# A planner's costs replaced by times read from the trace: block-sparse attention and a mixture of experts on one core

## The chip, the core and the metric

The kernel runs on one core of a Trainium2 chip. Five engines run their own instruction streams in order: TensorE (PE, with its weight loads PEld), VectorE (DVE), ScalarE (ACT), GpSimd (POOL) and SyncE (SP, which here only issues DMAs). They meet at semaphores. The metric is the device time of one execution in microseconds; lower is better.

## The reference

Attention over 4 batches x 8 heads, 768 positions of width 64, in blocks of 32: a query block sees its neighbours, the first and the last block, and three sampled blocks. Its output is the input x (3072 tokens x 512) of eight experts, whose outputs are weighted by a matrix P that is balanced by eight rounds of row and column division.

```
scores = np.where(mask, scale * q @ k.T, -1e9)
attn = exp(scores - max) / (sum + 1e-9);  x = attn @ v        # 3072 x 512
P = balance(exp(x @ w_gate - max))                            # 8 rounds, 3072 x 8
for e in range(8):
    h = np.maximum(x @ w1[e], 0.0)                            # 512 -> 1024
    out += P[:, e:e+1] * (h @ w2[e])                          # 1024 -> 512
```

## The kernel before

Every matrix operand is split into a high and a low half-precision part, and a product is three matmuls (high x high, high x low, low x high). The first 416 us are attention, whose order is written out by hand. After that come 32 items, item i = 4e + b being expert e on batch b. An item has two stages. Stage 1 (x @ w1) and stage 2 (h @ w2) each use a Strassen-like scheme of 7 products p = 0..6, and from expert 2 on four of stage 1's products are themselves split into 7 (L1620, groups of six matmuls of 192 columns; L1591 are the unsplit groups of six of 384 columns). Stage 2 is L1943, groups of twelve matmuls of 256 columns.

PE writes a bank of PSUM (p for stage 1, y for stage 2), DVE and ACT empty it and add it to sums in SBUF, and the same bank then takes the next product, so that a PE group often waits for the reader of the group before: L1573 (ACT), L1564, L1657, L1673, L1686, L1695 (DVE) in stage 1, L1970 (ACT) and L1982 (DVE) in stage 2. The relu'd sums are split again into h tiles: high parts by ACT (L1820), low parts by DVE (L1811, L1826, L1835) or POOL (L1809). Differences of sums are L1851, on DVE or POOL.

Stage 2's results of experts 2 to 6 are added to DRAM by an accumulating DMA that POOL issues (L2003, accd<-acc).

**A round of weights.** For each expert's w1 and w2 the kernel needs one power of two as a scale. ACT takes eight maxima (L352), DVE joins them (L441, ma_w<-mx_w), SP sends the 128 maxima to DRAM (L1316, peak_d<-ma_w) and reads them back to all partitions (L1320, peaks<-peak_d), and DVE makes the scale from them (L447 to L454, six small instructions in one job called power). Then ACT and DVE split the weights (L1346 and L1351). There are 15 such rounds after attention.

**Who sets the order.** Class Plan takes 7951 jobs with their dependencies, buffers and assumed durations, and runs through them in an assumed time: an engine that is free takes the ready job that is due first (PE: the one with the earliest place in a table of due times). What it yields is the program's order on each engine; at run time every engine keeps to that order, and only semaphores hold it. So an assumed time that is wrong doesn't change what is computed, but it places an instruction too early or too late in its engine's queue. Assumed are: LAT between engines, DMA_LAND from a DMA's last byte to its reader, MARGIN on durations. EASE, SHIFT, SLK and SLK2 set the due times of PE groups and of bank readers. A job with `port=True` doesn't run beside another such job in the plan: these are DVE's and POOL's jobs that read two operands from SBUF.

Of the kernel before, what the change touches and what calls it, by code (L numbers as in the profile page):

```python
# [32 lines left out]
PORDER = (0, 1, 5, 6, 3, 4, 2)  # L33
TWO = (6, 3, 1, 2)
NB1, NH, NPAIRS, NU, NACC = 5, 24, 9, 4, 3
SLK, SLK2, SHIFT, EASE, SOON = 1.5, 2.0, 9.5, 0.3, 120.0
SLK3 = 20.0
PREP0, PREP1, PREPD = 100, 190, 50
TWO1 = ()
ADDS = 2  # L40
LOFT = 31
# [16 lines left out]
class Job:  # L58
    __slots__ = (
        "engs", "fn", "deps", "take", "drop", "pt", "dl", "stream", "kb",  # L60
        "rush", "lag", "port", "wait", "succ", "start", "end", "eng", "ready", "seq", "free",
    )


class Plan:
    LAT = 0.2
    DMA_RATE, DMA_LAND = 190.0, 2.0
    MARGIN = 1.0

    def __init__(self, shelf):  # L70
        self.shelf = shelf
# [31 lines left out]
        self.jobs.append(j)  # L103
        return j

    def dma(self, fn, kb, deps=(), take=(), drop=(), dl=None, eng="SP"):
        return self.job({eng: 0.08 if eng == "SP" else 1.0}, fn, deps, take, drop, dl=dl, kb=kb)

    def engine(self, nc):
        return nc.gpsimd if self.current == "POOL" else nc.vector  # L110

    def span(self, j):
        if j.kb:
            return j.kb / self.DMA_RATE + self.DMA_LAND
        return min(j.engs.values())

    def deadlines(self):
# [11 lines left out]
    def run(self):  # L129
        self.deadlines()  # L130
        ENG = ("PE", "DVE", "ACT", "POOL", "SP", "-")
        free = {e: 0.0 for e in ENG}
        dma_free = 0.0
# [14 lines left out]
        wait = {}  # L148
# [40 lines left out]
        def start(j, e, t):  # L189
            nonlocal dma_free, port_free, left  # L190
            for h in j.take:
                if h.tile is None:
                    _, h.tile = items[h.pool].pop(0)
            j.start, j.eng = t, e
            dur = j.engs[e]
            if e not in ("PE", "SP", "-"):
                dur *= self.MARGIN
            if j.kb:
                begin = max(t + dur, dma_free)
                dma_free = begin + j.kb / self.DMA_RATE  # L200
                j.end = dma_free + self.DMA_LAND
                free[e] = t + dur
            else:
                j.end = t + dur
                free[e] = j.end
                if j.port:
                    port_free = j.end
            if e == "-":
                free[e] = 0.0
            for h in j.drop:  # L210
                h.users.discard(j)
                if not h.users:
                    items[h.pool].append((j.end + self.LAT, h.tile))
                    items[h.pool].sort(key=lambda x: x[0])
            if j.stream:
                pos[j.stream] += 1
            for s in j.succ:
                s.wait -= 1
                if not s.wait:
                    s.ready = max(  # L220
                        d.end + (self.LAT if d.eng != "-" and not (d.eng in s.engs and not d.kb) else 0.0)
                        for d in s.deps
                    ) + s.lag
                    cand.append(s)
            cand.remove(j)
            self.done.append(j)
            left -= 1

        EPSI = 1e-7
        while left:  # L230
            moved = False
            for e in ENG:
                while free[e] <= t + EPSI:
# [20 lines left out]
                    else:  # L254
                        for j in sorted(ok, key=lambda j: (j.dl, j.seq)):
                            end = t + j.engs[e]
# [42 lines left out]
def tile_sparse_attention_moe(  # L299
# [11 lines left out]
    nc = tc.nc  # L311
# [990 lines left out]
    def scale_jobs(which, e, loaded):  # L1302
        cell = {}

        def make():
            cell["steps"] = scale_steps(which, e)
            wr["s", which, e] = wr["s", which]

        made = job({"-": 0.0}, make, (loaded[1],))
        parts = [  # L1310
            job({"ACT": 0.81}, lambda k=k: cell["steps"][0][k](), (made, loaded[k // 4]))
            for k in (4, 5, 6, 7, 0, 1, 2, 3)
        ]
        whole = job({"DVE": 0.16}, lambda: cell["steps"][1](), parts)
        out_ = plan.dma(
            lambda: nc.sync.dma_start(out=peak_d[which - 1], in_=cell["steps"][4]), 1, (whole,)  # L1316
        )

        def back():
            nc.sync.dma_start(  # L1320
                out=peaks[which - 1],
                in_=peak_d[which - 1].rearrange("p one -> (p one)").unsqueeze(0).to_broadcast([P, P]),
            )
            wr["all", which] = peaks[which - 1]

        in_ = plan.dma(back, 64, (out_,))
        power = job({"DVE": 1.2}, lambda: cell["steps"][3](), (in_,))
        scaled[which, e] = power
        return parts, power
# [569 lines left out]
    def stage2(i, t0, length):  # L1899
# [99 lines left out]
        if e < NE - 1:  # L1999
            for j in range(2):  # L2000
                if fresh and e:
                    accstore[i, j] = plan.dma(
                        lambda j=j: nc.gpsimd.dma_start(  # L2003
                            out=accd[b][j], in_=pieces[j].tile, accum_op=ALU.add
                        ),
                        768, tuple(writes[j]) + (accstore[i - B, j],), drop=(pieces[j],), eng="POOL",
                    )
                else:
                    accstore[i, j] = plan.dma(
                        lambda j=j: nc.sync.dma_start(out=accd[b][j], in_=pieces[j].tile), 768,  # L2010
                        tuple(writes[j]), drop=(pieces[j],),
                    )
# [126 lines left out]
```

## Time and profile before

| | us |
|---|---|
| median of 3 runs | 2186.05 (2181.29 to 2190.05) |
| the profiled execution | 2180.49, span 2178.6 |
| PE busy | 2117.1 (97%) |
| DVE busy | 1714.8 (79%) |
| ACT busy | 1443.4 (66%) |
| POOL busy | 1202.2 (55%) |
| chain that ended last: PE 87%, DVE 6%, DMA 4% | |
| of it peak_d<-ma_w 2%, peaks<-peak_d 1% | |

The span is the time from the first to the last instruction of the profiled execution. PE's busy time is the union of its matmuls, so what is missing to the span is time in which PE had nothing running. The chain is followed back from the last instruction to whatever released it; a DMA on it means that at that place everything later stood behind that DMA. Times in the rows are counted from the span's start.

### The profile page before, as it was taken

How to read it: one execution, taken by the hardware profiler on the slowest of the kernel's cores; microseconds unless marked ns; L12 is line 12 of the kernel's file. 1: busy time of each engine (PE TensorE's matmuls, PEld its weight loads, DVE VectorE, ACT ScalarE, POOL GpSimd, SP SyncE). 2: the span in 40 equal slices, each digit the busy share in tenths (PEclk: the TensorE clock that was granted, in tenths of full speed). 3: DMA queues.
4: the chain of work that ended last, by engine and by line, in shares of the span. 5: the costliest groups of instructions: out<-in, count | busy, mean ns of one | idle time of the engine just before them, and what ended most of it. 6: DMA issues, size and time to landing. Idle time of an engine off the chain costs nothing.

```text
span 2178.6 us, 51353 instructions
## 1 busy us (share of the span) xinstructions
PE 2117.1 (97%) x20605; PEld 1708.3 (78%) x20605; DVE 1714.8 (79%) x3053; ACT 1443.4 (66%) x2773; POOL 1202.2 (55%) x1383
## 2 busy tenths in 40 slices
PE   6999999899999999999999999999999999999999
PEld 3777776667777778788888888888888888887887
DVE  8888888678787878777887688768876887787776
ACT  4788888776668656765676667656766676666442
POOL 5556768555445536554664466545654664475433
PEclk9999999999999999999999999999999999999999
DMA  7667966433456544564456454545464545455421
GB/s 171 142 135 163 211 132 137 141 106 104 154 176 193 168 158 131 151 150 110 120 139 150 110 148 128 133 110 143 118 148 110 146 131 132 110 163 147 139 95 66
DMA packets 228195, 300.57 MB, mean 138 GB/s; under 512 B 137436, under 2 KB 157812, under 8 KB 227956
## 3 DMA queue, kind: packets, MB, share of 16 engines
q1 hardware_dynamic: 221632, 265.80, 42.6%
q0 software_dynamic: 5760, 31.46, 8.7%
q8 instruction: 161, 2.64, 0.5%
q14 instruction: 78, 0.64, 0.1%
q10 hardware_dynamic: 564, 0.03, 0.0%
HBM read 198.15 MB, written 67.64 MB: 122 GB/s over the span
## 4 chain that ended last, share of the span: by engine, by line
PE 87%; DVE 6%; DMA 4%; issue 1%; ACT 1%; POOL 0%; SPq 0%; DVEq 0%; ACTq 0%; POOLq 0%
PE y L1943 38%; PE p L1591 21%; PE p L1620 14%; PE u L966 4%; PE t L904 2%; PE t L901 2%; PE m L868 2%; PE m L871 2%; DMA peak_d<-ma_w 2%; DMA peaks<-peak_d 1%; DVE top L877 1%; DMA qt<-qs 1%; PE u L997 0%; DVE pair L1851 0%; DVE pl L919 0%
## 5 line engine op out<-in xcount | busy, mean ns | idle before, releaser
L1943 PE MATMUL y<-w2p,h 128*128 128x256 f16 x8064 | 971.5, 273 | 5.1 <-ACT w2p L1346 2.1
L1943 PEld LDWEIGHTS <-h 128*128 128x128 f16 x8064 | 787.4, 98 | 126.3 <-issue 3.9
L1809 POOL TENSOR_TENSOR h<-pair,h 128x384 f16<-128x384 f32 x413 | 414.8, 1025 | 442.0 <-ACT h L1820 371.6
L1820 ACT ACTIVATE h<-pair 128x384 f16<-128x384 f32 x640 | 313.2, 515 | 79.4 <-DVE pair L1851 25.6
L1591 PE MATMUL p<-arena 128*128 128x384 f16 x1728 | 324.5, 327 | 0.6 <-DVE pair L1564 0.6
L1564 DVE SCALAR_TENSOR_TENSOR pair<-p,pair 128x384 f32<-128x384 f32 x384 | 212.9, 555 | 137.0 <-PE p L1591 132.4
L1805 ACT ACTIVATE pair<-pair 128x384 f32<-128x384 f32 x384 | 196.6, 518 | 165.9 <-DVE pair L1564 134.1
L1982 DVE SCALAR_TENSOR_TENSOR acc<-y,spare,acc 128x256 f32<-128x256 f32 x408 | 201.6, 496 | 114.1 <-PE y L1943 112.8
L1591 PEld LDWEIGHTS <-arena 128*128 128x128 f16 x1728 | 167.1, 98 | 83.1 <-issue 2.4
L877 DVE TENSOR_REDUCE top<-m 128x1 f32<-128x768 f32 x192 | 181.9, 951 | 48.7 <-PE m L871 47.8
L1591 PE MATMUL p<-attic 128*128 128x384 f16 x1152 | 216.4, 328 | 3.5 <-DVE pair L1564 3.5
L909 ACT ACTIVATE pe<-t,qk 128x768 int32<-128x768 f32 x192 | 172.3, 899 | 70.7 <-PE t L904 63.2
L1620 PEld LDWEIGHTS <-loft 128*128 128x128 f16 x2304 | 198.4, 98 | 25.2 <-issue 11.1
L1591 PEld LDWEIGHTS <-attic 128*128 128x128 f16 x1344 | 131.2, 98 | 73.5 <-issue 7.1
L1620 PE MATMUL p<-loft 128*128 128x192 f16 x1728 | 176.6, 246 | 1.9 <-DVE u L1657 1.1
L1970 ACT ACTIVATE acc<-y,spare 128x256 f32<-128x256 f32 (+1 forms) x180 | 97.7, 543 | 99.8 <-PE y L1943 99.2
L1851 POOL TENSOR_TENSOR pair<-pair,pair 128x384 f32<-128x384 f32 x114 | 126.4, 1119 | 59.1 <-DVE pair L1851 51.7
L1334 POOL TENSOR_TENSOR raw_w<-raw_w 128x256 f32<-128x256 f32 (+1 forms) x150 | 127.8, 862 | 56.1 <-DVE attic L1351 24.2
L1573 ACT ACTIVATE u<-p 128x384 f32<-128x384 f32 x216 | 105.3, 488 | 71.7 <-PE p L1620 68.4
L1809 POOL TENSOR_TENSOR h<-u,h 128x384 f16<-128x384 f32 x116 | 112.8, 978 | 67.4 <-ACT h L1820 60.1
L868 PE MATMUL m<-kt,qt 128*128 128x512 f16 (+1 forms) x384 | 126.6, 330 | 10.4 <-DMA kt<-ks 7.0
L1573 ACT ACTIVATE pair<-p 128x384 f32<-128x384 f32 x168 | 82.0, 489 | 82.0 <-PE p L1620 38.9
(236 smaller groups left out, 3937.7 us busy)
## 6 DMA issues: line engine op xcount, KB each, us to landing
arena<-xd SPq DMA_DIRECT2D x128, 384.0 KB, 3.3
attic<-xd SPq DMA_DIRECT2D x96, 384.0 KB, 3.3
loft<-xsd SPq DMA_DIRECT2D x96, 384.0 KB, 4.5
accd<-acc POOLq DMA_DIRECT2D x40, 768.0 KB, 8.5
raw_w<-in_moe_w_dram SPq DMA_DIRECT2D x28, 1024.0 KB, 5.2
accd<-acc SPq DMA_DIRECT2D x16, 768.0 KB, 4.2
acc<-accd SPq DMA_DIRECT2D x16, 768.0 KB, 5.1
xd<-loft SPq DMA_DIRECT2D x28, 384.0 KB, 2.9
```

The costliest lines, as they stand in the source:

```text
L868: nc.tensor.matmul(sc[:, lo:hi], lhsT=qt[:, 0, c], rhs=ka[:, lo:hi], start=True, stop=False)
L877: nc.vector.tensor_reduce(out=tops[n][:, c : c + 1], in_=sc[:, :S], axis=AX.X, op=ALU.max)
L909: nc.scalar.activation(pe, sc[:, :S], AF.Exp, bias=EXP_SHIFT, scale=qk[n // 2][3])
L1564: lambda: nc.vector.scalar_tensor_tensor(out=out_(), in0=bank_(), scalar=HDOWN, in1=add(), op0=ALU.mult, op1=ALU.add),
L1573: lambda: nc.scalar.activation(out_(), bank_(), AF.Relu if relu else AF.Copy, scale=HDOWN),
L1591: nc.tensor.matmul(bk.tile[:, :TH], lhsT=w1p[p][:, l, kc, fs], rhs=xp[p][:, r, kc], start=(fresh and kc == 0 and m == 0), stop=(kc == KH - ...
L1620: nc.tensor.matmul(bk.tile[:, c * HT : (c + 1) * HT], lhsT=lhs(l, c), rhs=rhs(rr), start=(fresh and c == 0 and m == 0), stop=(m == 2), ski ...
L1805: return job({"ACT": 0.52}, lambda: nc.scalar.activation(view(), view(), AF.Relu), dep)
L1809: nc.gpsimd.tensor_tensor(out=out_, in0=x, in1=y, op=ALU.subtract)
L1820: lambda: nc.scalar.activation(h.tile[:, 0], src(), AF.Relu if relu else AF.Copy),
L1943: nc.tensor.matmul(py, lhsT=hh[i, p, kc].tile[:, l, tsl], rhs=w2p[p][:, r, kc], start=(old is None and kc == 0 and m == 0), stop=(kc == h2 ...
L1982: lambda dst=dst, src=src, t=t: nc.vector.scalar_tensor_tensor(out=dst(), in0=src(), scalar=pwe[e][:, t : t + 1] if e else 1.0, in1=dst(), ...
```

## The change

The planner's assumed times are replaced. LAT falls from 0.2 to 0.06 us; every duration on DVE, ACT and POOL is multiplied by 1.08; an engine is free again 0.08 (DVE), 0.1 (ACT) or 0.06 us (POOL) before its job ends; a DMA has its own landing time, 8.0 us for peak_d<-ma_w, 5.2 for peaks<-peak_d, 4.5 for the accumulating DMA and 2.0 for the rest. The due times change through SLK, SLK2, SHIFT and EASE. PREP0 is used only for products in TWO1, which is empty. No job is added or removed: the same 7951 jobs are put in another order, and 51 more of those that DVE or POOL may take fall to DVE (25 from L1809 to L1811, 26 of L1851), while of the preparation of x two, net, go the other way. Attention's order is the same on every engine.

```diff
--- before.py
+++ after.py
@@ -33,9 +33,9 @@
 PORDER = (0, 1, 5, 6, 3, 4, 2)
 TWO = (6, 3, 1, 2)
 NB1, NH, NPAIRS, NU, NACC = 5, 24, 9, 4, 3
-SLK, SLK2, SHIFT, EASE, SOON = 1.5, 2.0, 9.5, 0.3, 120.0
+SLK, SLK2, SHIFT, EASE, SOON = 2.5, 5, 11, 0.2, 120.0
 SLK3 = 20.0
-PREP0, PREP1, PREPD = 100, 190, 50
+PREP0, PREP1, PREPD = 60, 190, 50
 TWO1 = ()
 ADDS = 2
 LOFT = 31
@@ -58,14 +58,15 @@
 class Job:
     __slots__ = (
         "engs", "fn", "deps", "take", "drop", "pt", "dl", "stream", "kb",
-        "rush", "lag", "port", "wait", "succ", "start", "end", "eng", "ready", "seq", "free",
+        "rush", "lag", "port", "land", "wait", "succ", "start", "end", "eng", "ready", "seq", "free",
     )
 
 
 class Plan:
-    LAT = 0.2
+    LAT = 0.06
+    OVER = {"DVE": 0.08, "ACT": 0.1, "POOL": 0.06}
     DMA_RATE, DMA_LAND = 190.0, 2.0
-    MARGIN = 1.0
+    MARGIN = 1.08
 
     def __init__(self, shelf):
         self.shelf = shelf
@@ -103,15 +104,17 @@
         self.jobs.append(j)
         return j
 
-    def dma(self, fn, kb, deps=(), take=(), drop=(), dl=None, eng="SP"):
-        return self.job({eng: 0.08 if eng == "SP" else 1.0}, fn, deps, take, drop, dl=dl, kb=kb)
+    def dma(self, fn, kb, deps=(), take=(), drop=(), dl=None, eng="SP", land=None):
+        j = self.job({eng: 0.08 if eng == "SP" else 1.0}, fn, deps, take, drop, dl=dl, kb=kb)
+        j.land = self.DMA_LAND if land is None else land
+        return j
 
     def engine(self, nc):
         return nc.gpsimd if self.current == "POOL" else nc.vector
 
     def span(self, j):
         if j.kb:
-            return j.kb / self.DMA_RATE + self.DMA_LAND
+            return j.kb / self.DMA_RATE + j.land
         return min(j.engs.values())
 
     def deadlines(self):
@@ -198,11 +201,11 @@
             if j.kb:
                 begin = max(t + dur, dma_free)
                 dma_free = begin + j.kb / self.DMA_RATE
-                j.end = dma_free + self.DMA_LAND
+                j.end = dma_free + j.land
                 free[e] = t + dur
             else:
                 j.end = t + dur
-                free[e] = j.end
+                free[e] = j.end - self.OVER.get(e, 0.0)
                 if j.port:
                     port_free = j.end
             if e == "-":
@@ -1313,7 +1316,7 @@
         ]
         whole = job({"DVE": 0.16}, lambda: cell["steps"][1](), parts)
         out_ = plan.dma(
-            lambda: nc.sync.dma_start(out=peak_d[which - 1], in_=cell["steps"][4]), 1, (whole,)
+            lambda: nc.sync.dma_start(out=peak_d[which - 1], in_=cell["steps"][4]), 1, (whole,), land=8.0
         )
 
         def back():
@@ -1323,7 +1326,7 @@
             )
             wr["all", which] = peaks[which - 1]
 
-        in_ = plan.dma(back, 64, (out_,))
+        in_ = plan.dma(back, 64, (out_,), land=5.2)
         power = job({"DVE": 1.2}, lambda: cell["steps"][3](), (in_,))
         scaled[which, e] = power
         return parts, power
@@ -2003,7 +2006,7 @@
                         lambda j=j: nc.gpsimd.dma_start(
                             out=accd[b][j], in_=pieces[j].tile, accum_op=ALU.add
                         ),
-                        768, tuple(writes[j]) + (accstore[i - B, j],), drop=(pieces[j],), eng="POOL",
+                        768, tuple(writes[j]) + (accstore[i - B, j],), drop=(pieces[j],), eng="POOL", land=4.5,
                     )
                 else:
                     accstore[i, j] = plan.dma(
```

What this does to the order is seen at three places. In the rows of the changed kernel lines up to L106 are one higher and the lines of the jobs three higher (L441 is L444, L447 is L450). The numbers behind names are buffers.

DVE in the last round (w2 of expert 7), before: the rows that stand behind L441 up to L447, which waits for peaks.

```order
L1982 SCALAR_TENSOR_TENSOR acc_8056<-y_8016,spare_24582,acc_8056 128x256
L1835 TENSOR_TENSOR h_8028<-p_8010,h_8028 128x384
L1982 SCALAR_TENSOR_TENSOR acc_8056<-y_8017,spare_24582,acc_8056 128x256
L1851 TENSOR_TENSOR pair_8047<-p_8010,pair_8047 128x384
L1564 SCALAR_TENSOR_TENSOR pair_8042<-p_8013,pair_8042 128x384
L1564 SCALAR_TENSOR_TENSOR pair_8042<-p_8014,pair_8042 128x384
L1686 SCALAR_TENSOR_TENSOR pair_8050<-p_8012,u_8052 128x2x192
L1826 SCALAR_TENSOR_TENSOR h_8022<-pair_8042,h_8022 128x384
L1982 SCALAR_TENSOR_TENSOR acc_8056<-y_8015,spare_24582,acc_8056 128x256
L1564 SCALAR_TENSOR_TENSOR pair_8048<-p_8013,pair_8048 128x384
L1564 SCALAR_TENSOR_TENSOR p_8013<-p_8013,pair_8043 128x384
L447 TENSOR_REDUCE ma_w_7_26855<-peaks_8069 128x1
```

The same place in the changed kernel: the first five and the last six of the rows behind L444, with 20 left out.

```order
L1567 SCALAR_TENSOR_TENSOR pair_8046<-p_8012,pair_8046 128x384
L1567 SCALAR_TENSOR_TENSOR p_8013<-p_8013,pair_8049 128x384
L1567 SCALAR_TENSOR_TENSOR p_8012<-p_8012,pair_8049 128x384
L1862 SCALAR_TENSOR_TENSOR u_8053<-p_8013,pair_8045 128x384
L1862 SCALAR_TENSOR_TENSOR u_8054<-p_8012,pair_8045 128x384
...
L1985 SCALAR_TENSOR_TENSOR acc_8056<-y_8015,spare_24653,acc_8056 128x256
L1698 SCALAR_TENSOR_TENSOR pair_8049<-p_8014,u_8051 128x2x192
L1567 SCALAR_TENSOR_TENSOR pair_8042<-p_8010,pair_8042 128x384
L1567 SCALAR_TENSOR_TENSOR p_8010<-p_8010,pair_8043 128x384
L1985 SCALAR_TENSOR_TENSOR acc_8056<-y_8016,spare_24653,acc_8056 128x256
L450 TENSOR_REDUCE ma_w_7_26851<-peaks_8069 128x1
```

Before, 11 rows stand between the maximum and the row that waits for the round trip; now 30 do.

SP at the same round, before: peak_d and peaks are the round trip, raw_w, xd and xsd are loads of weights and of x.

```order
L475 DMA attic<-xd_77 128x1536
L1498 DMA loft<-xsd_8071 128x1536
L475 DMA arena<-xd_77 128x1536
L1316 DMA peak_d_8067<-ma_w_7_26855 128x1
L1320 DMA peaks_8069<-peak_d_8067 128x128
L475 DMA arena<-xd_77 128x1536
```

SP there in the changed kernel.

```order
L478 DMA attic<-xd_77 128x1536
L1501 DMA loft<-xsd_8071 128x1536
L1319 DMA peak_d_8067<-ma_w_7_26851 128x1
L478 DMA attic<-xd_77 128x1536
L1501 DMA loft<-xsd_8071 128x1536
L478 DMA arena<-xd_77 128x1536
L1323 DMA peaks_8069<-peak_d_8067 128x128
```

Before, the read stands straight behind the write; now three loads of x stand between them.

POOL behind the accumulating DMA of item 12's first half (expert 3, batch 0), before; raw_w is a weight buffer.

```order
L2003 DMA accd_0_8058<-acc_8055 128x1536
L1809 TENSOR_TENSOR h_8026<-pair_8042,h_8026 128x384
L1809 TENSOR_TENSOR h_8030<-pair_8050,h_8030 128x384
L1809 TENSOR_TENSOR h_8021<-pair_8047,h_8021 128x384
L1851 TENSOR_TENSOR pair_8048<-pair_8048,pair_8050 128x384
```

The same DMA in the changed kernel.

```order
L2006 DMA accd_0_8058<-acc_8055 128x1536
L1812 TENSOR_TENSOR h_8023<-pair_8043,h_8023 128x384
L1337 TENSOR_TENSOR raw_w<-raw_w 128x512
L1854 TENSOR_TENSOR pair_8044<-pair_8044,pair_8042 128x384 x2
L1812 TENSOR_TENSOR h_8032<-pair_8043,h_8032 128x384
L1812 TENSOR_TENSOR h_8026<-pair_8042,h_8026 128x384
L1812 TENSOR_TENSOR h_8027<-pair_8044,h_8027 128x384
L1812 TENSOR_TENSOR h_8022<-pair_8049,h_8022 128x384
```

The DMA is followed by three h rows and a difference before, and by one h row, a weight sum (L1337), two differences and four h rows now.

## Rows read from the trace of the kernel before

**Rows 1.** Windows before and from the plan: stretch, length, busy per engine, granted clock.

```profile
0.00:416.00 416.00, 388.35 (x5324) 278.00 (x5324) 344.33 (x561) 321.60 (x441) 265.58 (x397) 0.99 0.71 158
416.00:2179.00 1763.00, 1728.71 (x15281) 1430.27 (x15281) 1370.51 (x2493) 1121.82 (x2332) 936.63 (x986) 1.00 0.47 133
```

**Rows 2.** PE's waits, 416 to 2179: waiter, releaser, total us, times, longest.

```profile
PE p L1620 <- DVE pair L1695: 7.7, 5, 2.9
PE p L1620 <- DVE u L1657: 7.6, 8, 1.4
PE p L1591 <- DVE pair L1564: 4.1, 2, 3.5
PE y L1943 <- ACT w2p L1346: 2.1, 1, 2.1
PE y L1943 <- DVE w2p L1351: 1.9, 2, 1.3
PE p L1591 <- DVE pair L1851: 1.5, 1, 1.5
PE p L1620 <- ACT pair L1573: 1.1, 1, 1.1
```

**Rows 3.** DVE's waits, 416 to 2179, the one row on L447.

```profile
DVE ma_w L447 <- DMA peaks<-peak_d: 36.4, 10, 6.7
```

**Rows 4.** The two small DMAs: form, count, KB each, median us to landing.

```profile
peaks<-peak_d SPq DMA_DIRECT2D x15, 64.0 KB, 5.4
...
peak_d<-ma_w SPq DMA_DIRECT2D x15, 0.5 KB, 7.3
```

**Rows 5.** Timeline of DVE, last round: start us, us, instruction, idle before.

```profile
1970.21 0.15 DVE L441 TENSOR_REDUCE ma_w<-mx_w 128x1 f32<-128x8 f32 x1
...
1978.08 0.56 DVE L1564 SCALAR_TENSOR_TENSOR p<-p,pair 128x384 f32<-128x384 f32 x1
1982.98 0.28 DVE L447 TENSOR_REDUCE ma_w<-peaks 128x1 f32<-128x128 f32 x1 [4.34 <-DMA peaks<-peak_d]
```

**Rows 6.** Chain of waits, 1955 to 1992: start us, us, what.

```profile
1970.38 7.11 DMA peak_d<-ma_w
...
1977.50 5.38 DMA peaks<-peak_d
```

**Rows 7.** Timeline of PE at three of the gaps.

```profile
1551.28 0.66 PE L1620 MATMUL p<-arena,loft 128*128 128x192 f16 x6 [2.35 <-DVE pair L1695]
...
1769.22 0.66 PE L1620 MATMUL p<-arena,loft 128*128 128x192 f16 x6 [1.56 <-DVE pair L1695]
...
1984.60 0.66 PE L1620 MATMUL p<-arena,loft 128*128 128x192 f16 x6 [2.94 <-DVE pair L1695]
```

**Rows 8.** Windows at the four drops of the granted clock.

```profile
448.40:455.30 6.90, 5.17 (x17) 2.48 (x17) 6.85 (x13) 4.74 (x9) 1.85 (x1) 0.56 0.48 176
905.80:909.20 3.40, 2.04 (x10) 1.33 (x10) 3.40 (x7) 3.40 (x7) 0.43 (x1) 0.63 0.50 202
1550.90:1554.30 3.40, 3.02 (x20) 2.54 (x20) 2.84 (x5) 3.26 (x5) 0.90 (x1) 0.63 0.42 107
1984.40:1987.80 3.40, 3.20 (x22) 2.61 (x22) 3.40 (x7) 3.40 (x5) 0.89 (x1) 0.63 0.44 120
```

**Rows 9.** Timeline of POOL, DVE and PE around one accumulating DMA.

```profile
1179.28 0.88 POOL L2003 DMA_DIRECT2D accd<-acc  x1 [2.55 <-PE y L1943]
...
1179.89 2.94 POOL L1809 TENSOR_TENSOR h<-pair,h 128x384 f16<-128x384 f32 x3
...
1180.19 3.07 DVE L1851 TENSOR_TENSOR pair<-pair,pair 128x384 f32<-128x384 f32 x1
...
1183.18 1.01 DVE L1657 SCALAR_TENSOR_TENSOR u<-p,pair 128x384 f32<-128x384 f32 x2
1183.78 0.41 PE L1620 MATMUL p<-loft,attic 128*128 128x192 f16 x3 [1.02 <-DVE u L1657]
```

**Rows 10.** DVE's h rows on L1811, from 420 us: count, busy us, mean ns, idle before.

```profile
L1811 DVE SCALAR_TENSOR_TENSOR h<-pair,h 128x384 f16<-128x384 f32 x99 | 77.2, 786 | 3.9 <-ACT h L1820 3.9
```

## The prediction, made before the result was known

> **What bounds the kernel now.** I read the page first: PE is busy for 97% of the span and makes up 87% of the chain that ended last, so the kernel is bound by matmul work that the change neither adds to nor takes from. What can move is PE's idle time, and the time that it spends at half clock. So the second view is windows at the seam between the hand-ordered attention and the planned part [rows 1]. Attention's order is the same on all engines, so its 27.7 us of idle PE stay. In the planned part PE is busy for 1728.7 of 1763.0 us: 34.3 us idle is nearly all that any order could win.
>
> The third view, PE's waits, says where they are [rows 2]: a few dozen gaps of 0.4 to 3.5 us, nearly all released by DVE, though DVE is busy for only 78% of that stretch (1370.5 of 1763.0). An engine with free time that releases late is itself held, so the fourth view is DVE's own waits [rows 3]: L447, the first instruction of the power job, holds DVE's queue ten times for 36.4 us in all, up to 6.7 us at once, until the second of two small DMAs has landed. The DMA view has their medians, 7.3 us for the write and 5.4 us for the read back [rows 4]. The planner of before counted about 2 us for each landing, so it placed power some 8 us too early in DVE's queue. The timeline of the last round shows what follows [rows 5]: DVE ends its last row before power at 1978.64, sits idle for 4.34 us, and the six small rows follow. The chain runs through just these two DMAs, 7.11 and 5.38 us [rows 6]. Behind power stands L1695, which empties the bank that PE needs next, and PE sits idle until 1984.60, for 2.94 us [rows 7].
>
> **What the waits on L447 cost PE.** I add the gaps that lie right behind such a hold. Three waits on L1695: 2.35 + 1.56 + 2.94 = 6.85 us [rows 7] (the row's total of 7.7 has two small ones more that lie elsewhere). Both waits on L1564, 4.1 us, behind the first round's hold of 6.7 us [rows 2, 3]. At about 906 the stage 2 of expert 2 waits for its freshly split weights, 2.1 us for the high and 1.3 us for the low part, and once, behind another round's hold, PE waits 1.1 us for ACT [rows 2]. Sum: 6.85 + 4.1 + 3.4 + 1.1 = 15.5 us.
>
> Four of these gaps are followed by a lower granted clock: windows of 6.9 and three times 3.4 us have means of 0.56 and 0.63 of full speed [rows 8], which is the lower level (1.2 GHz) but for the windows' edges. PE was idle just ahead and for part of each. Busy time multiplied by the missing share of the clock is 5.17 x 0.44 + (2.04 + 3.02 + 3.20) x 0.37 = 2.3 + 3.0 = 5.3 us.
>
> **The change part by part.** The new landing times, 8.0 and 5.2, are close to the medians. In the new order 30 DVE rows stand between L441 and L447 in the last round, where 11 stood. At about 0.56 us each [rows 5] they are 17 us of DVE work, against a round trip of 7.11 + 5.38 = 12.5 us [rows 6]; DVE's waits for PE come on top. Every later round of w2 has 30 rows too, so these holds should go whole. The first round has 24 rows, 13.4 us against 12.7 by the medians: thin. The rounds of w1 get 25 to 28 rows (it was 21 to 24), some 15 us, and may still hold DVE; before, no gap of PE followed theirs directly. What hides the longer round is that weights are needed later: in the new order the first split of w2 and its user still have several PE groups between them, about as many as before. SP now issues three loads of x between write and read. Each can hold SP's queue while x is still being read by PE, which delays the read at worst until the next group of PE is done; the spare is 17 - 12.5 = 4.5 us. I count 15.5 + 5.3 = 20.8 us as removed, less 2 for what the first round and expert 2 may keep: 19 us. Both ends: 10 (half of the gaps are the matmuls' own lateness and come back) and 21.
>
> The other waits: LAT, MARGIN, the overlaps and the due times reshuffle every queue. What is left after 15.5 of 34.3 us is mainly the eight waits on L1657, 7.6 us, and one of 1.5 on L1851 [rows 2]; the rest is small gaps and the end of the kernel, where the order still closes with the same 26 groups of stage 2. Five of the waits on L1657 look alike [rows 9]. POOL waits 2.55 us to issue an accumulating DMA, then runs three h rows back to back (1179.89 to 1182.83). A DVE difference that also reads two SBUF operands starts at 1180.19 and lasts 3.07 us. L1657, behind it, starts at 1183.18, and PE has been idle for 1.02 us. The new order has such places too: behind the same DMA more POOL rows stand in a row, though no DVE row with two SBUF operands stands beside them there; elsewhere one does. I take this term as 0, with -8 (all gone) and +12 (twice as many and longer) as ends.
>
> The 51 jobs that fall to DVE are 51 x 0.79 = 40 us of it [rows 10], about what the holds give back (36.4), so DVE stays near 78%. If that cover is gone, DVE is at 80%, and the bank readers come later by a fraction of a row; I keep it within the +12.
>
> The Trainium skill, page "SBUF — State Buffer", section "SBUF: two separate sides", says of these two engines that their shared pair of ports is locked for one instruction, and that whoever comes second blocks fully for that instruction. By that rule a DVE row would lose one POOL row at most, about 1 us. In this trace it lost three [rows 9]: the measurement decides. By the rule alone the slower rival below would fall away; by the row it lives.
>
> Sum: 2180.5 - 19 = 2161.5 for an execution like the profiled one. That one was 5.6 us faster than the median of the three runs; from the median the sum is 2167. I take the middle, 2164 us. Its own range, from the ends 10 and 21 and from -8 to +5 of the small waits, is 2152 to 2177.
>
> **The rivals.**
> First, the gaps move instead of going. PE's waits on L1695 are replaced by waits behind POOL's bursts, or the power job, now late, makes the splits late. For it: the new order has up to five POOL rows ready behind an accumulating DMA, and 40 of these DMAs. Against: only eight waits on L1657 in 40 before, each about 1 us. If twelve more such gaps of 1.2 us come, 14 us of the 19 are lost: 2181 us.
>
> Second, the times fit so much better that the collisions go as well. For it: DVE's holds make the run drift from the plan, and the collision of [rows 9] is one that the plan forbids (`port`). Against: POOL's waits for DVE's sums stay. Then 8 + 2 us more are won: 2154 us.
>
> Third, slower: a DVE row with two SBUF operands meets a burst of five POOL rows instead of three. The hold grows from 3.07 to about 5 us and PE's gap from 1.02 to 3 us; gaps of 2.35 and 2.94 us were followed by a lower clock [rows 7, 8], about 1.1 us more each. With two such places per expert in five experts: 10 x 4.1 = 41, less the 7.6 there now, less the 19 won: +14 us, 2200 us. It decides from about ten such gaps on. For it: the new order puts a low part on DVE and a difference of sums at the end of such a burst once per item or two. Against: the plan keeps these jobs apart.
>
> **How the numbers follow.** The forecast has 0.63, the second rival 0.12, the first 0.15, the third 0.10. A measurement of this kernel can tell 0.5%, 11 us, from no change: faster is below 2175, slower above 2197. The forecast falls into "no change" with one part in twenty or so of its chance, and the first rival lies there with nearly all of its own, while the second is faster: faster 0.72, same 0.18, slower 0.10. For 8 times in 10 I go from 2150, a little under the second rival, to 2184, beyond the first.
>
> **What would show it.** In the changed kernel's profile: the wait of DVE on L450 (L447 of before) falls from 36.4 us to under 15, and what is left is in the rounds of w1. PE's waits on L1698 and L1567 (L1695 and L1564 of before) fall from 11.8 to under 3 us. The granted clock stays at full speed but for one drop at most after 430 us. PE's idle time from 416 us on falls from 34 to about 19 us, and the two small DMAs' share of the chain from 3% to under 1%. The forecast is wrong if PE's total of waits on DVE's L1660 (L1657) is above 15 us, if DVE rows of 3 us and more number above ten, or if stage 2 waits for w2p at every expert.

## The result, and the profile after

The changed kernel takes 2158.8 us (median of 4 runs, 2156.38 to 2162.62) beside 2183.67 for the kernel before on the same chip (2180.62 to 2190.05): a ratio of 0.9884, interval 0.9856 to 0.9912. That is 25 us or 1.2% less, and the runs of the two kernels don't overlap. The profiled execution took 2156.38 us with a span of 2154.6, 24.0 us shorter than the profiled span before. Line numbers of the new kernel are 3 higher: L447 is now L450, L1620 is L1623, L1657 is L1660, L1695 is L1698.

The windows at the same seam, with the same columns as [rows 1]:

```profile
0.00:416.00 416.00, 388.72 (x5342) 278.42 (x5342) 345.66 (x564) 321.29 (x441) 265.50 (x397) 1.00 0.71 159
416.00:2155.00 1739.00, 1720.79 (x15263) 1425.83 (x15263) 1390.99 (x2539) 1110.60 (x2332) 897.03 (x937) 1.00 0.52 135
```

Up to the end of the last instruction, PE's idle time after 416 us fell from 33.9 to 17.8 us and its busy time by 7.9 us. Not all of this is the change's. Attention, whose order is the same, runs 1.8 us ahead in this execution: the first matmul on xn starts at 416.16 us instead of 417.92, and 18 matmuls that stood behind 416 us now stand before it (both traces have 20605). From that matmul on, before and after:

```profile
417.92:2178.60 1760.68, 1727.99 (x15263) 1429.68 (x15263) 1369.53 (x2489) 1121.82 (x2332) 936.63 (x986) 1.00 0.47 133
416.16:2154.60 1738.44, 1720.79 (x15263) 1425.83 (x15263) 1390.89 (x2538) 1110.60 (x2332) 897.03 (x937) 1.00 0.52 135
```

So the planned part gave 22.2 of the 24.0 us, for the same 15263 matmuls: 15.0 of idle time (32.7 to 17.7) and 7.2 of busy time.

PE's waits after 416 us (waiter, releaser, total us, times, longest), to be held against [rows 2]:

```profile
PE p L1623 <- DVE pair L1854: 3.4, 1, 3.4
PE p L1623 <- DVE u L1660: 3.2, 6, 2.0
PE y L1946 <- DVE h L1829: 2.6, 6, 0.5
PE p L1623 <- DVE pair L1676: 1.8, 1, 1.8
PE p L1594 <- DVE pair L1567: 1.4, 2, 0.7
...
PE p L1623 <- DVE pair L1698: 0.6, 1, 0.6
```

DVE's own wait at the start of power, which was 36.4 us in ten holds [rows 3]:

```profile
DVE ma_w L450 <- DMA peaks<-peak_d: 2.3, 1, 2.3
```

The waits on L1698 and L1567, 11.8 us before, are 2.0; those on the fresh w2p are gone. The hold is left once, in a round of w1. The two small DMAs themselves show no sign of being faster (form, count, KB, median us to landing; before [rows 4]):

```profile
peaks<-peak_d SPq DMA_DIRECT2D x15, 64.0 KB, 8.5
...
peak_d<-ma_w SPq DMA_DIRECT2D x15, 0.5 KB, 8.7
```

These medians, 17.2 us together where it was 12.7, are over the landings that the profile knows: in after those of 3 writes and 7 reads of 15, and all seven are reads of w1's rounds. In before the reads of the same seven rounds had a median of 8.7 us. The DMAs no longer show because more DVE work stands in front of power. The timeline of DVE in the last round, where before 4.34 us of idle stood ahead of power [rows 5]:

```profile
1940.36 0.15 DVE L444 TENSOR_REDUCE ma_w<-mx_w 128x1 f32<-128x8 f32 x1
...
1959.35 0.48 DVE L1985 SCALAR_TENSOR_TENSOR acc<-y,spare,acc 128x256 f32<-128x256 f32 x1 [0.28 <-PE y L1946]
1959.75 0.28 DVE L450 TENSOR_REDUCE ma_w<-peaks 128x1 f32<-128x128 f32 x1
```

From the maxima to power it is now 19.4 us of DVE's time, and power follows the row before it without a gap.

Of gaps of 1 us and more PE has four after 416 us, where it had 13: 3.40, 2.03, 1.80 and 1.07. The first two, from PE's timeline (start us, us, instruction, idle before):

```profile
897.38 2.44 PE L1623 MATMUL p<-loft 128*128 128x192 f16 x18 [3.40 <-DVE pair L1854]
...
1974.15 0.66 PE L1623 MATMUL p<-loft,attic 128*128 128x192 f16 x6 [2.03 <-DVE u L1660]
```

The window at the first of them holds the one drop of the granted clock after 430 us, where there were four [rows 8]:

```profile
897.00:900.40 3.40, 3.02 (x23) 2.91 (x23) 2.89 (x5) 1.54 (x3) 3.00 (x3) 0.65 0.15 58
```

Neither gap is a wait for a DMA. At the first, DVE works without a pause from 890.87 us on: a split of w2 (1.27 us), the job that weighs an expert's tokens (1.7 us) and seven other rows stand ahead of the one that PE needs, L1854. It is the round of w2 of expert 2, where before had its gaps at about 906 [rows 8]. DVE's timeline just ahead of the second gap:

```profile
1968.91 0.20 DVE L1468 TENSOR_SCALAR pc<-iw,iw 128x1 f32<-128x1 f32 x1
1969.15 3.80 DVE L1470 TENSOR_SCALAR pcb<-inv_v,pc 128x4 f32<-128x4 f32 x1
...
1973.56 0.55 DVE L1660 SCALAR_TENSOR_TENSOR u<-p,pair 128x384 f32<-128x384 f32 x1
```

and POOL's at the same time:

```profile
1968.41 0.88 POOL L2006 DMA_DIRECT2D accd<-acc  x1 [0.59 <-PE p L1623]
1969.02 1.21 POOL L1812 TENSOR_TENSOR h<-u,h 128x384 f16<-128x384 f32 x1
1969.89 1.20 POOL L1812 TENSOR_TENSOR h<-pair,h 128x384 f16<-128x384 f32 x1
1970.77 1.28 POOL L1854 TENSOR_TENSOR pair<-pair,pair 128x384 f32<-128x384 f32 x1
1971.72 1.19 POOL L1812 TENSOR_TENSOR h<-pair,h 128x384 f16<-128x384 f32 x1
```

A DVE row over four columns (part of the same weighing job), 0.23 us at its shortest, runs for 3.80 us, as long as a train of POOL rows without gaps, and the reader of PE's bank stands behind it. Such a place I call a meeting below. It is of the kind of [rows 9].

### The profile page after: what moved, and what is told of

It reads as the page before. It is cut to its first block, busy times and chain, and to the rows that moved or that the text cites. A ratio compares the mean times of both kernels' runs of the same rounds, so it can differ in the third digit from the quotient of the medians.

```text
span 2154.6 us, 51373 instructions
## 1 busy us (share of the span) xinstructions
PE 2109.5 (98%) x20605; PEld 1704.2 (79%) x20605; DVE 1736.7 (81%) x3102; ACT 1431.9 (66%) x2773; POOL 1162.5 (54%) x1334
## 4 chain that ended last, share of the span: by engine, by line
PE 91%; DVE 5%; issue 1%; ACT 1%; DMA 1%; POOL 1%; SPq 0%; ACTq 0%; POOLq 0%; DVEq 0%
PE y L1946 40%; PE p L1594 23%; PE p L1623 14%; PE u L969 4%; PE t L904 2%; PE t L907 2%; PE m L871 2%; PE m L874 2%; DVE top L880 1%; DVE h L1829 1%; DVE pcb L1470 1%; DMA qt<-qs 1%; PE u L1000 0%; DVE pl L922 0%; ACT pe L912 0%
## 5 line engine op out<-in xcount | busy, mean ns | idle before, releaser
L1812 POOL TENSOR_TENSOR h<-pair,h 128x384 f16<-128x384 f32 x386 | 396.4, 1036 | 456.3 <-ACT h L1823 381.8
L1567 DVE SCALAR_TENSOR_TENSOR pair<-p,pair 128x384 f32<-128x384 f32 x384 | 213.5, 556 | 153.5 <-PE p L1594 150.0
L1623 PEld LDWEIGHTS <-loft 128*128 128x128 f16 x2304 | 199.5, 98 | 18.2 <-issue 6.7
L1623 PE MATMUL p<-loft 128*128 128x192 f16 x1728 | 180.3, 247 | 5.4 <-DVE pair L1854 3.4
L1337 POOL TENSOR_TENSOR raw_w<-raw_w 128x256 f32<-128x256 f32 (+1 forms) x150 | 131.0, 884 | 33.4 <-DVE attic L1354 14.3
L871 PE MATMUL m<-kt,qt 128*128 128x512 f16 (+1 forms) x384 | 127.2, 331 | 10.3 <-DMA kt<-ks 7.0
L926 POOL TENSOR_SCALAR pl<-pe 128x768 f16<-128x768 uint16 x112 | 96.3, 864 | 70.7 <-ACT pe L912 68.6
L904 PE MATMUL t<-qt,kt 128*128 128x512 f16 (+1 forms) x384 | 125.5, 327 | 2.8 <-DVE top L880 2.1
```

Of the source, the lines that this page charges most:

```text
L871: nc.tensor.matmul(sc[:, lo:hi], lhsT=qt[:, 0, c], rhs=ka[:, lo:hi], start=True, stop=False)
L904: nc.tensor.matmul(sc[:, lo:hi], lhsT=kt[:, 0, c], rhs=qa[:, lo:hi], start=True, stop=False)
L1567: lambda: nc.vector.scalar_tensor_tensor(out=out_(), in0=bank_(), scalar=HDOWN, in1=add(), op0=ALU.mult, op1=ALU.add),
L1623: nc.tensor.matmul(bk.tile[:, c * HT : (c + 1) * HT], lhsT=lhs(l, c), rhs=rhs(rr), start=(fresh and c == 0 and m == 0), stop=(m == 2), ski ...
L1812: nc.gpsimd.tensor_tensor(out=out_, in0=x, in1=y, op=ALU.subtract)
```

## The experiments

The theory was: DVE's queue is held at power by the two small DMAs, PE waits for the bank readers behind it, and the new landing times put enough DVE work ahead of it. The rivals were that the other new times or the new due times make the gain, and that any new order of 7951 jobs falls somewhere in a spread, by luck. Each ratio is to the kernel before, run in the same rounds on the same chip (its medians 2183.67 to 2188.28 us). "Hold" is DVE's wait at power, "idle" PE's idle time after 416 us, in the profiled execution. That one can lie off the median: e9's is 7.5 us above it, e7's and e11's are the quickest of ten.

| kernel | us | ratio, interval | idle | hold (times) |
|---|---|---|---|---|
| before | | 1 | 33.9 | 36.4 (10) |
| after | 2158.80 | 0.9884, 0.9856 to 0.9912 | 17.8 | 2.3 (1) |
| e5: order of before, no wait | 2163.43 | 0.9893, 0.9866 to 0.9920 | 23.6 | 1.4 (1) |
| e1: landing times alone | 2159.68 | 0.9871, 0.9851 to 0.9891 | 22.1 | 0 |
| e2: all but landing times | 2218.55 | 1.0149, 1.0120 to 1.0179 | 62.6 | 41.2 (8) |
| e7: e2's order, no wait | 2183.45 | 0.9996, 0.9984 to 1.0007 | 36.5 | 5.7 (2) |
| e6: order of after, no wait | 2157.05 | 0.9859, 0.9838 to 0.9879 | 18.7 | 0 |
| e3: durations and distances alone | 2240.11 | 1.0254, 1.0239 to 1.0269 | 75.7 | 65.8 (14) |
| e4: due times alone | 2166.07 | 0.9912, 0.9898 to 0.9927 | 23.9 | 25.5 (7) |
| e10: landing, durations, distances | 2170.07 | 0.9920, 0.9903 to 0.9938 | 27.3 | 2.2 (2) |
| e11: landing and due times | 2181.90 | 0.9974, 0.9958 to 0.9990 | 33.8 | 0.3 (1) |
| e8: after and port on the weighing | 2150.34 | 0.9843, 0.9829 to 0.9858 | 11.8 | 0 |
| e9: e1 and port on the weighing | 2182.00 | 0.9976, 0.9952 to 0.9999 | 36.6 | 0 |
| e12: e11 and port on the weighing | 2174.13 | 0.9941, 0.9924 to 0.9959 | 28.2 | 1.5 (3) |

**The wait alone (e5).** The order of before stays as it is; power reads a constant tile that was loaded long ago, so it waits for no read back, and the scales are those of the constant. The DMAs still run.

```diff
-            wr["all", which] = peaks[which - 1]
+            wr["all", which] = ident
```

> The kernel before in its own order, but the scale's first instruction reads a constant 128x128 tile instead of the tile that the round trip brings, so it waits for no DMA; the DMAs still run. (The scales are those of the constant.) Theory 1: all ten holds of DVE go, and with them PE's 15.5 us of gaps and the drops of the clock: about 2162 us, 18 to 24 us less than before, ratio 0.989 to 0.992; PE's waits on L1657 (7.6 us) stay. Theory 2: under 8 us less, ratio above 0.996.

Without the wait the kernel is 23.9 us faster, with the same instructions in the same order on every engine: the holds are the cause, shown. No drop of the granted clock is left after 430 us. The one wait at power that stays, 1.4 us, is for the write, which still reads the maxima that power overwrites. (By the profiled spans, 2178.6 and 2161.3, it is 17.3: 10.3 of idle time and 7.0 of busy time. The profiled execution of before was one of its quicker ones.) The waits behind the meetings stay as they were [rows 2], and that at L1564 falls from 4.1 to 0.6 and at L1695 from 7.7 to 1.0 us. PE's waits in e5:

```profile
PE p L1620 <- DVE u L1657: 7.6, 8, 1.4
PE y L1943 <- DVE w2p L1351: 3.5, 2, 2.9
...
PE p L1620 <- DVE pair L1695: 1.0, 3, 0.6
PE p L1591 <- DVE pair L1564: 0.6, 1, 0.6
```

The second row holds a new gap of 2.90 us, at 1773.98. The gaps at about 906 are gone. DVE's timeline of e5 at the new one:

```profile
1767.70 6.23 DVE L1351 SCALAR_TENSOR_TENSOR w2p<-raw_w,sw,w2p 128x1024 f16<-128x1024 f32 x1
1773.85 0.55 DVE L1686 SCALAR_TENSOR_TENSOR pair<-p,u 128x384 f32<-128x384 f32 x1
```

and POOL's there:

```profile
1767.50 1.04 POOL L1809 TENSOR_TENSOR h<-pair,h 128x384 f16<-128x384 f32 x1
1768.37 0.85 POOL L1334 TENSOR_TENSOR raw_w<-raw_w 128x256 f32<-128x256 f32 x1
```

The same three instructions in the kernel before:

```profile
1783.84 1.86 DVE L1351 SCALAR_TENSOR_TENSOR w2p<-raw_w,sw,w2p 128x1024 f16<-128x1024 f32 x1
```

```profile
1783.63 0.97 POOL L1809 TENSOR_TENSOR h<-pair,h 128x384 f16<-128x384 f32 x1
1784.51 1.78 POOL L1334 TENSOR_TENSOR raw_w<-raw_w 128x256 f32<-128x256 f32 x1
```

In both kernels DVE's split (1.28 us where it is alone) begins 0.2 us behind the same POOL row. Before, it took 1.86 us, and POOL's next row was the one that waited, 1.78 us instead of 0.85. In e5 it took 6.23 us, as long as POOL's train of six rows from 1767.50 to 1772.84 and the split itself. So the hold had not kept the two engines apart, and the rows don't show what decides between one POOL row and a whole train.

**The landing times alone (e1).** Only `land=8.0` and `land=5.2` are set in the planner of before; LAT, MARGIN, the overlaps, the due times and the accumulating DMA's landing stay as they were.

```diff
-        ... out=peak_d[which - 1], in_=cell["steps"][4]), 1, (whole,)
+        ... out=peak_d[which - 1], in_=cell["steps"][4]), 1, (whole,), land=8.0
-        in_ = plan.dma(back, 64, (out_,))
+        in_ = plan.dma(back, 64, (out_,), land=5.2)
```

> The kernel before with the new landing times of the two small DMAs alone (8.0 and 5.2 us); LAT, MARGIN, overlaps, due times and the accumulating DMA's landing stay as before. Between the maximum and the scale's first instruction now stand 21 to 56 DVE rows per round (10 to 14 before in the rounds of w2, now 21 to 37). Theory 1 (the gain is the hold of DVE behind the round trip): DVE's wait on that instruction falls from 36.4 us to under 12, PE's idle time in the planned part from 34 to about 20, time 2160 to 2170 us, ratio 0.990 to 0.994. Theory 2 (the gain comes from the whole new order, its closer durations and due times): ratio 0.996 to 1.000, since the gaps come back elsewhere.

Two numbers alone give as much as the whole change: 0.9871 beside 0.9884, with intervals that overlap, and a little more than theory 1 had (2160 to 2170 us). PE's idle time is 22.1 and not 17.8 us, its busy time 1719.64 beside 1720.79, and none of its gaps is over 1.8 us.

**All but the landing times (e2), and the same without the wait (e7).** e2 is the changed kernel with e1's two lines put back as they were in before; the accumulating DMA keeps its 4.5.

```diff
-        in_ = plan.dma(back, 64, (out_,), land=5.2)
+        in_ = plan.dma(back, 64, (out_,))
```

> The changed kernel with the landing times of the two small DMAs set back to 2.0 us; everything else as changed. Between the maximum and the scale stand 7 to 29 DVE rows in most rounds, as few as 7 or 8 in three. Theory 1: DVE is held again for 30 to 45 us in all, PE idles for 30 us and more in the planned part, 2175 to 2190 us, ratio to the kernel before 0.996 to 1.003. Theory 2: it keeps most of the gain, 2158 to 2166 us, ratio 0.989 to 0.992.

e2 is slower than before by 31.2 us, far outside both ranges I expected. The hold in e2, and the waits of PE:

```profile
DVE ma_w L450 <- DMA peaks<-peak_d: 41.2, 8, 8.8
```

```profile
PE p L1594 <- DVE pair L1567: 9.8, 2, 9.1
PE p L1623 <- DVE pair L1676: 8.9, 5, 3.2
PE p L1623 <- DVE pair L1854: 8.7, 6, 3.0
```

The hold is only a little longer than before's 36.4 us, yet PE loses far more. So e7 takes the wait out of e2's order as e5 did (the scales are again those of the constant):

> The changed kernel without the two landing times (2218.6 us when it waits for the round trip), in that very order, but the scale's first instruction reads a constant 128x128 tile and waits for no DMA. (The scales are those of the constant.) Theory 1: its loss is the holds of DVE and what they set off, so it falls by 45 to 60 us, to 2158 to 2173 us. Rival: the tighter order is bad in itself, and it stays above 2190 us.

It comes to 2183.45 us, between the two ranges I expected, and 1.3 below before: of the 56 us between e2 and after (+31.2 and -24.9) the wait is about 32.5, and 23.6 belong to the order itself. In e7 eight DVE rows of the planned part are longer than 2.2 us, up to 5.8, and gaps of 15.6 us in all begin beside one or within 3 us behind it. (The hold of 5.7 us is again for the write.)

**The wait taken from after (e6).** The same edit as in e5, in the new kernel:

> The same edit in the changed kernel: its order, but no wait for the round trip. The changed kernel holds DVE once, for 2.3 us. Theory 1: no more than 2 us faster than the changed kernel, 2155 to 2160 us. A rival: the round trip still costs the changed kernel something that the holds don't show (the splits start late), then 2150 us or less.

2157.05 us, 0.9859: its interval overlaps after's, and the idle time is 18.7 beside 17.8. Nothing is left to win from these DMAs.

**The durations and distances alone (e3), the due times alone (e4).** Each sets the values of one of these two lines (written here in short) in the planner of before, and no landing times:

```diff
+    LAT, MARGIN = 0.06, 1.08;  OVER = {"DVE": 0.08, "ACT": 0.1, "POOL": 0.06}     # e3
+SLK, SLK2, SHIFT, EASE, SOON = 2.5, 5, 11, 0.2, 120.0                             # e4
```

> The kernel before with LAT 0.06, MARGIN 1.08 and the engines' overlaps of the change, and nothing else (due times and all landing times as before). Between the maximum and the scale's first instruction stand 9 to 28 DVE rows, 9 to 14 in the rounds of w2. Theory 1 (the round trip alone decides): DVE is held for 40 us or more, 2185 to 2215 us, ratio 0.999 to 1.013. Theory 2 (closer times are a gain by themselves): ratio 0.990 to 0.996.

> The kernel before with the new SLK, SLK2, SHIFT and EASE alone. Between the maximum and the scale stand 11 to 32 DVE rows; from the eighth round on the rounds of w2 have 13 to 25. Theory 1: by the rows, holds of 15 to 30 us in all, 2170 to 2190 us, ratio 0.992 to 1.001. Theory 2 (the due times carry the loss of the kernel that has all but the landing times, 2218 us): ratio above 1.007.

e3 is the slowest kernel of all, 55.4 us over before; I expected 2215 us at most. The hold, and PE's waits in e3:

```profile
DVE ma_w L450 <- DMA peaks<-peak_d: 65.8, 14, 9.0
```

```profile
PE p L1623 <- DVE pair L1676: 24.0, 9, 3.8
PE p L1623 <- DVE pair L1698: 21.6, 7, 7.0
```

Here between 9 and 28 DVE rows stand between the maxima and power, 12 at the median; in before it is 10 to 76, 21 at the median, in after 24 to 40, 30 at the median. e4 wins 18.6 us, more than I expected, with 25.5 us of hold left:

```profile
DVE ma_w L450 <- DMA peaks<-peak_d: 25.5, 7, 6.4
```

No single wait of PE in e4 is above 3.2 us. That due times with more slack let PE run ahead of the bank readers, so that a hold costs less, is my reading; no run shows it by itself. A microsecond of hold has no fixed price: before 36.4 us of it went with 33.9 of idle, in e4 25.5 with 23.9, in e2 41.2 with 62.6.

**Two of three parts together (e10, e11).** e10 sets the three landing times with e3's line, e11 with e4's.

> The two landing times together with LAT, MARGIN and the overlaps of the change, due times as before. The closer times alone cost 55 us (2240.1 us) and held DVE for 65.8 us. Now 15 to 37 DVE rows stand between the maximum and the scale. Theory 1 (their loss is the holds): no hold beyond 5 us in all, 2155 to 2168 us. Rival (the closer times pack PE too tightly in any case): above 2175 us.

> The two landing times together with the new due times (and the accumulating DMA's landing), LAT, MARGIN and overlaps as before: 18 to 69 DVE rows between the maximum and the scale. Theory 1: no holds, so within 5 us of the changed kernel, 2153 to 2162 us; the closer times are then worth nothing. Rival: the closer times are needed too, 2166 us (what the due times give alone) or more.

Both have next to no hold, and both are slower than the two landing times alone: 2170.07, between the two ranges I expected, and 2181.90, with the rival. (They also have the accumulating DMA's landing time, which e1 has not; it was not run by itself.) So the parts do not add, and with the holds gone something else spreads the orders by more than 30 us. In e11 PE waits mostly here:

```profile
PE p L1623 <- DVE pair L1676: 13.9, 10, 2.1
PE p L1623 <- DVE u L1660: 8.4, 5, 2.2
```

DVE has 17 rows longer than 2.2 us in e11; four of them come three times each, one expert apart: 3.58 (L1829), 3.9 (L1854), 2.54 (L1470, the weighing) and 2.5 us (L1354, a split).

**The meeting of the weighing with POOL (e8, e9, e12).** The job with L1470 reads only SBUF, but is not among those that the plan keeps from running beside POOL's. The edit marks it, in after (e8), in e1 (e9) and in e11 (e12):

```diff
-        weighed[e] = job({"DVE": 1.0}, fn, tuple(deps) + (scaled[1, e], scaled[2, e]))
+        weighed[e] = job({"DVE": 1.0}, fn, tuple(deps) + (scaled[1, e], scaled[2, e]), port=True)
```

> The changed kernel with one edit: the job of L1468 to L1472 (three small DVE instructions that weigh P for the next expert) is marked port=True, so the planner keeps it from standing beside a POOL job that reads two SBUF operands. In the changed kernel L1470, of 128x4 elements, takes 0.23 us at best, 2.0 at the median and 3.8 at most, and its longest stands just ahead of PE's gap of 2.03 us. Theory: that gap goes and the median of L1470 falls under 0.5 us; 1 to 4 us faster than the changed kernel, 2155 to 2158 us. Rival: the new order moves other collisions into its place, within 2 us of the changed kernel.

e8 is the fastest kernel found: 2150.34 us, 0.9843 of before, 8.5 us under after where I expected 1 to 4. The line L1470 in e8 (count, min/median/max ns, first and last start) and in after:

```profile
L1470 DVE TENSOR_SCALAR pcb<-inv_v,pc x8: 229/626/952, 549.2 to 1963.6; 128x4 f32<-128x4 f32 x8
```

```profile
L1470 DVE TENSOR_SCALAR pcb<-inv_v,pc x8: 232/1996/3798, 546.5 to 1969.1; 128x4 f32<-128x4 f32 x8
```

No DVE row of its planned part is longer than 2.2 us (after has 11). The gap of 2.03 us at 1974 and that of 1.80 are gone, that at 897 is 2.27 instead of 3.40: 4.96 of the 6.0 us by which idle time fell. Only the first of the three stood behind a long row of L1470, and only one of after's 11 long rows is L1470's: the mark moved other jobs as well, and their meetings went with them.

> The kernel before with the two landing times (2159.7 us by themselves) and the weighing job marked port=True. Theory (the mark takes away meetings of DVE and POOL in any order): no DVE row of 3 us and more, PE's idle time from 22 to about 14 us, 2148 to 2156 us. Rival (the 8.5 us that the mark gave in the changed kernel are luck of that order): 2157 us or more.

> The same with the weighing job marked port=True. Theory: the mark again takes 5 to 9 us off, and the kernel is as fast as the marked changed kernel (2150.3 us) or faster, 2146 to 2153 us. Rival: the mark changes less than 3 us here.

In e1's order the same mark costs about 22 us: my expectation failed. Other jobs moved here too, and in three experts a split of w2 now meets a train of POOL rows. DVE's timeline of e9 at the first:

```profile
1132.97 6.25 DVE L1354 SCALAR_TENSOR_TENSOR w2p<-raw_w,sw,w2p 128x1024 f16<-128x1024 f32 x1
1139.15 0.55 DVE L1660 SCALAR_TENSOR_TENSOR u<-p,pair 128x384 f32<-128x384 f32 x1
```

and what PE waits for there, and in all:

```profile
1139.74 1.12 PE L1623 MATMUL p<-loft 128*128 128x192 f16 x6 [3.50 <-DVE u L1660]
```

```profile
PE p L1623 <- DVE u L1660: 15.3, 10, 3.6
```

The other two rows take 6.27 us at 1357 and 6.3 at 1577, each with a gap of 3.5 us behind it. In e11's order the mark wins 7.8 us (e12), as expected, but the kernel stays 24 us above e8, which I expected it to reach. So the mark is worth what the meetings are worth that it happens to leave, and the rival of luck holds for this part: with next to no hold left, orders lie between 2150 and 2182 us. That the meetings are the cause of this spread is read from rows: the gaps counted as in e7 are 0 in e8, 5.9 us in after, 8.0 in e1, 8.2 in e10, 17.8 in e12, 21.3 in e11 and 15.0 in e9. No kernel took the meetings away with the order kept, so how much of it they are stays open.

## Why the prediction was right

**The forecast** was 2164 us, with a range of its own from 2152 to 2177; 2158.8 lies in it, on the low side. From the profiled execution the forecast counted 19 us, and 24.1 came, of which 1.8 lie in attention and are no effect of the change.

**The holds.** The step said 15.5 us of gaps behind them, with 2 us kept. The same lines of PE's waits now hold 2.0 us, so 13.5 went, as the sum had it (15.5 less 2). e5 shows that the holds were the cause of the largest of them, and e1 that the landing times take them away. What failed in detail: the hold fell to 2.3 us, further than "under 15"; six other rounds, those whose landing the profile knows, have 3.4 to 5.8 us to spare. The cover was counted against 12.5 us, the round trip of the last round, or 12.7 by the medians. In the rounds of w1 of experts 3 to 6 it was 18.0 to 18.7 us already in before, and it is 18.3 in the one round that is still held. The rows of DVE were mis-sized as well: the 28 rows of a round of w1, "some 15 us" in the prediction, take 22.7 us at 1167, and the 30 of the last round 19.4 instead of 17, since DVE waits for PE among them. The two errors cancel nearly everywhere, which is luck. (The row counts of the prediction hold from expert 3 on; in the rounds ahead of that there are 24 to 40.)

**The clock.** Four drops became one, as said. The term was 5.3 us for all four, and PE's busy time fell by 7.2 from the seam on. The step was mis-sized: it multiplied a window's busy time by the share of clock that the window missed on average, in windows that begin ahead of the drops. The four stretches at the lower level in before, at their own bounds, and the one in after:

```profile
449.29:456.12 6.83, 5.99 (x19) 2.84 (x19) 6.78 (x12) 3.89 (x9) 1.85 (x1) 0.50 0.43 146
906.67:910.09 3.42, 2.66 (x13) 1.85 (x13) 3.42 (x8) 3.36 (x7) 1.10 (x1) 0.50 0.51 208
1551.79:1555.21 3.42, 3.42 (x20) 2.68 (x18) 1.95 (x3) 3.28 (x6) 0.90 (x1) 0.50 0.65 199
1985.29:1988.70 3.41, 3.41 (x20) 2.63 (x18) 2.67 (x6) 3.41 (x6) 1.01 (x2) 0.50 0.69 158
```

```profile
898.05:901.46 3.41, 3.41 (x23) 3.04 (x22) 2.75 (x5) 1.01 (x2) 2.42 (x3) 0.50 0.00 0
```

At half the full clock, half of the busy time is the loss: 15.48 / 2 = 7.7 us before, 1.7 after, so 6.0 net. The remaining 1.2 us I can't place.

**The small waits** were taken as 0 between -8 and +12, and came to -1.5 (15.0 less 13.5). It is a balance: those on L1660 fell from 7.6 to 3.2 us, while those on L1854 rose from 1.5 to 3.4, those on L1676 from 0.8 to 1.8, and 2.6 on L1829 are new. So the 22.2 us of the planned part are 13.5 + 6.0 + 1.5 and the 1.2 that I can't place. The prediction's bound for it was sound; its sign was chance, as the spread from e1 to e12 shows.

**DVE's load.** It is busy for 80% of the planned part (1390.99 of 1739), not for 78: the jobs that fell to it do show. They cost no PE time that the rows tell.

**The rivals.** The first (gaps move) came about only once: there are four gaps of 1 us and more in place of 13, but the largest, 3.40 us, lies in the round of before's gaps at about 906. The second (collisions go as well) was half right: fewer, and one more mark in the plan (e8) brings 2150.34 us, below that rival's 2154. The third, slower, needs about ten gaps of some 3 us behind such meetings, and after has one of 2.03. But its mechanism is real: e9 has ten waits on L1660, three of them of 3.5 us, and lost all but 6 us of e1's gain.

On these meetings the Trainium skill, page "SBUF — State Buffer", section "SBUF: two separate sides", has the shared ports locked for one instruction at a time. The split at 1783.84 in before agrees: it waited for one POOL row, and POOL's next one waited for it. In e9 a DVE row of 1.27 us lasted 6.25 beside a train of POOL rows, and in after one of 0.23 us lasted 3.80: the measurement decides, and the wait can be for the whole train.

**What was not foreseen at all** is how much the rest of the change costs without its first part: with e3's durations and distances the median of the rows ahead of power falls from 21 to 12, and the holds rise from 36.4 to 65.8 us. Which of LAT, MARGIN and OVER does it was not run. The two landing times alone give the 25 us and repair what e3's line does, but they are not the only way: the due times alone gave 18.6.

## What to carry to other kernels

When an engine with free time releases late, look at its own queue for an instruction that waits for a DMA, and put as much work ahead of it as the DMA's measured round trip takes, with some spare. Measure it at each place: in before it was 11 to 14 us in the rounds of w2 and about 18 in those of w1 of experts 3 to 6. Model the largest wrong time first: a plan made tighter everywhere, with these landing times still at 2 us, was the worst of all. After that, orders differ by chance encounters of engines, so a mark or a cost that wins in one order must be measured again in the next.

## What the runs showed of the hardware that was not expected

- A DVE instruction that reads only SBUF can be held for a whole train of POOL rows: 0.23 us became 3.80 in after (128x4), 1.28 became 6.23 in e5 and 6.25 in e9 (128x1024), while the POOL rows beside it in after grew only from 0.92 to between 1.19 and 1.28 us. It isn't the rule: in before, from 416 us on, 155 DVE rows are more than 0.2 us longer than the shortest of their line, tiles and shape, and 142 of them by less than 1.1 us.
- The same meeting can go either way: beginning 0.2 us behind the same POOL row, the same split took 1.86 us in before and 6.23 in e5.
- The landing of a small DMA is not set by its size alone: in before the 64 KB read took 4.1 to 6.5 us in eleven rounds and 8.7 to 9.4 in four, and the 0.5 KB write 7.0 to 9.3 in the twelve rounds whose landing the profile knows, while the 384 KB loads in the planned part took 3.3 to 4.5 us by their medians. What else sets it, no run separates.
